# An expert's remaining tiles in a six-arm branch, with the arm told to TensorE beforehand

## The chip, the core and the metric

The kernel runs on one core of a Trainium2 chip. The core has five engines that work side by side and wait for each other by semaphores: TensorE (PE; its weight loads are listed apart as PEld), VectorE (DVE), ScalarE (ACT), GpSimd (POOL) and SyncE (SP). Each engine takes its instructions, branches among them, from its own queue. The time is in microseconds on the device, from one execution of the whole program; less is better.

## What is computed

Sliding-window causal attention (8 batches, 8 heads, 576 positions, head size 64, window 64) makes 4608 rows of 512. A mixture of 8 experts then works on them: each row goes to the one expert with the highest logit, and no row is dropped.

```python
scores = where(0 <= i - j < 64, q @ k.T / 8, -1e9)
x = (softmax(scores) @ v) -> [4608, 512]
logits = x @ w_gate                       # [4608, 8]
e = argmax(logits, 1);  gate = softmax(logits)[e]
out = gate * (relu(x @ w1[e]) @ w2[e])    # w1 512x1024, w2 1024x512, in float32
```

How many rows an expert gets is known only when the routing is done, on the chip.

## The kernel before

The attention runs first, over 16 units of two batches and two heads. Its rows go to memory (`x_dram`), their gates are folded in, and the routing (`choose`, `starts`, `slot_table`) builds a list of rows ordered by expert (`perm_i`). An expert's rows are handled in tiles of 256 slots (`TB`). A tile is either *full* (`hidden` and `output`: one level of Strassen-like products, seven for each of the two layers) or, where at most 160 slots are left, a *half tile* (`half_tile`: plain products on 160 slots).

`starts` (L215) works out for each expert how many full tiles (`fulls_i`) and how many tiles of any kind (`all_i`) it has, eight numbers each in `info_i`. `loads` (L870) brings them into registers of every engine. Expert 0 always has its first two tiles done ahead of the loop (`NE`), as `tile0` and `tile1`; each other expert has at least one, taken as full.

The order within the loop is written out by hand (`manual_schedule`). `body` (L481) is one tile. Its first steps belong to the tile before: `finish` (L422, the last three additions on VectorE) and `scatter` (L287, two indirect DMAs by GpSimd into the result). Then come, where given, sums of weights on GpSimd (`between`: four instructions at L139), the products, the transposes of the next tile's rows on VectorE (L311), and `gather` (L268, two indirect DMAs by GpSimd that bring the rows of the tile after the next). So the data of a tile are gathered two tiles ahead, and TensorE can begin a tile while VectorE finishes the one before.

For each expert the loop issues the loads of the next expert's weights on SyncE (L1060, L1061), does `body` for the first tile (not for expert 0), and calls `more` for the rest. `more(n)` (L1068) is a chain of nested conditions: is there a tile n (L1070)? Is it full (L1071)? If full, the body and then `more(n + 1)` inside; else the half tile and out. From the fourth tile on a loop takes over. Every engine goes through these branches on its own. Where a path is not taken, its semaphore counts are made up for at the branch (on GpSimd the records INC_SWDGE_SEM and the waits ahead of them), so that the code that follows can wait for one number whatever the path. Nothing in the nested conditions is announced to an engine ahead of the branch.

Of the kernel before, what the change touches and what calls it, by code (L numbers as in the profile page):

```python
# [13 lines left out]
I32 = mybir.dt.int32  # L14
AF = mybir.ActivationFunctionType
ALU = mybir.AluOpType
# [20 lines left out]
def kernel(  # L37
# [29 lines left out]
    NE = 2  # L67
# [3 lines left out]
    KT = 4  # L71
# [16 lines left out]
    wg = consts.tile([P, NG, GE], F32, name="wg")  # L88
    nc.gpsimd.memset(wg[:], 0.0)
    perm_i = consts.tile([P, NS], I32, name="perm_i")  # L90
    info_i = consts.tile([P, 2, E], I32, name="info_i")
    fulls_i, all_i = info_i[:, 0], info_i[:, 1]

    places_i = consts.tile([P, E + 1], I32, name="places_i")
    perm_e = consts.tile([P, NE * C], I32, name="perm_e")
# [119 lines left out]
    def starts():  # L215

        for got, slots in ((fulls_i, TB - 1 - HALF), (all_i, TB - 1)):
            V.tensor_scalar(out=got, in0=count[:], scalar1=float(slots), scalar2=float(TB), op0=ALU.add, op1=ALU.max)
            V.tensor_single_scalar(got, got, TB.bit_length() - 1, op=ALU.arith_shift_right)
        V.tensor_copy(out=nt[:], in_=all_i)  # L220
        V.tensor_tensor_scan(out=cum[:], data0=ones[:, 0:E], data1=nt[:], initial=0.0, op0=ALU.mult, op1=ALU.add)
        V.tensor_tensor(out=start[:], in0=cum[:], in1=nt[:], op=ALU.subtract)
        V.tensor_single_scalar(chunk0[:], start[:], float(C), op=ALU.mult)
# [273 lines left out]
    with tc.manual_schedule(), ExitStack() as held, ExitStack() as brief:  # L497
# [372 lines left out]
        def loads():  # L870

            both_ = lambda t: t[0:1].rearrange("p a e -> p (a e)")
            _, n = nc.values_load_multi_w_load_instructions(both_(info_i), min_val=0, max_val=NT // P)
            _, places = nc.values_load_multi_w_load_instructions(
                places_i[0:1, :], engines=(mybir.EngineType.Pool,), min_val=0, max_val=NTILE
            )
            return [(n[e], n[E + e], places[e]) for e in range(E)], places[E]

        def after(s, routing, bg):

# [173 lines left out]
    with tc.manual_schedule():  # L1054
        load_w1(1)
        load_w2(1)
        for e in range(E):
            fulls, tiles, first = regs[e]
            if 0 < e < E - 1:
                load_w1(e + 1)  # L1060
                load_w2(e + 1)  # L1061
            def place(i):
                i = nc.s_assert_within(
                    first + i, 0, NTILE - 1, skip_runtime_bounds_check_because="a tile with a token is one of the NTILE"
                )
                return bass.ds(i * C, C), bass.ds((i + 3) * C, C)

            def more(n, between=None):  # L1068

                with tc.If(tiles > n) as some_left:  # L1070
                    with tc.If(fulls > n, preferred_fallthrough_block=False) as full:  # L1071
                        body(e, *place(n), True, between)
                        if n + 1 < KT:
                            more(n + 1)
                        else:
                            with tc.For_i(KT, fulls) as i:
                                body(e, *place(i), True)
                            with tc.If(tiles > fulls):
                                body(e, *place(fulls), False)
                    with full.Else():  # L1080
                        body(e, *place(n), False, between)
                if between is not None:
                    with some_left.Else():
                        between()

            if e:
                body(e, *place(0), True, partial(sums_w2, e))
            more(1 if e else NE, partial(sums_w1, e + 1) if e + 1 < E else None)
        finish()
        scatter(perm_i[:, bass.ds(end * C, C)])  # L1090

# [27 lines left out]
```

## Time and profile before

| what | value |
|---|---|
| three runs | 742.86, 746.24 and 747.09 us; median 746.24 us |
| the profiled execution | 741.95 us, of which the profile's span is 740.2 us |
| granted TensorE clock, mean | 0.975 |
| attention, routing and the first two tiles of expert 0 | 0 to about 272 us |
| the expert loop | about 272 to 728 us |
| from TensorE's last product to the end | 728 to 740 us |
| PE, PEld, DVE, ACT, POOL busy | 94, 84, 67, 36, 48% of the span |

A line of a group or of the timeline reads: engine, line of the kernel, operation, what it writes and reads (partitions x elements), how often, and in brackets the idle time of the engine ahead of it with what released it. "issue" means that the engine waited for nothing that the profile shows. A q behind an engine's name means its queue's own instructions, branches among them, which are not counted as busy. TensorE's queue works ahead of its matmuls.

### The profile page before, as it was taken

Reading aid. Unit: us, or ns where it says so; the run is one execution under the profiler, and the core shown is the slowest. Engines: PE = TensorE matmul, PEld = TensorE weight load, DVE = VectorE, ACT = ScalarE, POOL = GpSimd, SP = SyncE. Lnnn points to the kernel's source line nnn. Section 1 sums busy time; section 2 is a strip of 40 time slices with the busy share of each in tenths; the row PEclk is TensorE's granted clock in tenths of the full one; section 3 lists DMA queues with packets and bytes.
Section 4 is the critical chain, followed back from the end, with each engine's and each line's share of the span. In section 5 each row is a group of like instructions: output and inputs, shape, how many; then the busy total and the mean of one; then the engine's idle time right before and its main releaser. Section 6 shows DMA issues by size and latency. Waiting matters only on the chain. (4 is left out here: it accounts for less than half of the span.)

```text
span 740.2 us, 18250 instructions
## 1 busy us (share of the span) xinstructions
PE 695.1 (94%) x6962; PEld 625.4 (84%) x6962; DVE 496.7 (67%) x1654; ACT 267.3 (36%) x676; POOL 355.7 (48%) x366
## 2 busy tenths in 40 slices
PE   4999999999799989999999999999899999989993
PEld 3888888888678978998999899899899899989892
DVE  2576898998848484765677568667466568556762
ACT  4788888897735111212122122112111222111220
POOL 5224659288680217676540555654167654262102
PEclk8899999999989999999999999999999999999997
DMA  8998879887524635336100630711422711101101
GB/s 160 218 210 188 182 179 228 192 212 214 176 55 143 205 109 180 127 107 228 59 29 31 220 124 18 271 59 43 174 110 78 253 60 28 61 9 59 33 27 57
DMA packets 137636, 94.68 MB, mean 128 GB/s; under 512 B 117072, under 2 KB 117072, under 8 KB 137490
## 3 DMA queue, kind: packets, MB, share of 16 engines
q1 hardware_dynamic: 127858, 62.16, 31.7%
q0 software_dynamic: 9056, 28.58, 11.8%
q10 hardware_dynamic: 576, 2.10, 1.0%
q8 instruction: 78, 1.28, 0.7%
q14 instruction: 68, 0.56, 0.3%
HBM read 73.94 MB, written 20.45 MB: 128 GB/s over the span
## 5 line engine op out<-in xcount | busy, mean ns | idle before, releaser
L311 DVE STREAM_TRANSPOSE v_m<-qk_m 32x256 f32<-32x256 f32 x320 | 139.3, 435 | 5.2 <-DMA qk_m<-x_dram,at_g 0.3
L340 PE MATMUL bank<-qk_m,s 128*128 128x128 f32 x1024 | 124.7, 278 | 0.6 <-issue 0.6
L271 POOL DMA_INDIRECT qk_m<-x_dram,at_g x42 | 45.0, 1072 | 165.0 <-DVE v_m L311 155.9
L340 PEld LDWEIGHTS bank<-qk_m,s 128*128 128x128 f32 x1024 | 120.6, 195 | 0.6 <-issue 0.6
L340 PE MATMUL bank<-qk_m,w 128*128 128x128 f32 x768 | 96.0, 279 | 11.8 <-issue 8.1
L340 PEld LDWEIGHTS bank<-qk_m,w 128*128 128x128 f32 x768 | 91.0, 194 | 15.9 <-issue 15.7
L652 ACT ACTIVATE pr<-pr,mx 128x128 f32<-128x128 f32 x288 | 89.7, 390 | 31.7 <-DVE mx L642 31.3
L642 DVE CUSTOM_DVE_ANT_0 pr<-bank,mask 128x128 f32<-128x128 f32 x288 | 64.4, 285 | 28.0 <-PE bank L629 26.7
L380 DVE TENSOR_TENSOR v_m<-bank,v_m 128x256 f32<-128x256 f32 x95 | 38.2, 420 | 55.3 <-PE bank L384 24.9
L291 POOL DMA_INDIRECT out_dram<-v_m,at_s x42 | 42.5, 1013 | 61.5 <-DVE v_m L380 47.2
L570 POOL COPY v_m<-v_m 64x520 f32<-64x520 f32 x32 | 19.8, 618 | 68.6 <-DMA v_m<-in_v_dram 58.3
L139 POOL TENSOR_TENSOR s<-w 128x1024 f32<-128x1024 f32 x22 | 52.2, 2373 | 0.0
L675 PEld LDWEIGHTS bank<-v_m,pT 128*64 128x64 f32 x1152 | 41.1, 140 | 10.9 <-DVE xs L689 4.8
L675 PE MATMUL bank<-v_m,pT 128*64 128x65 f32 x1152 | 47.8, 231 | 1.9 <-DVE xs L689 1.9
L347 ACT COPY qk_m<-bank 128x512 f32<-128x512 f32 x16 | 9.4, 586 | 108.2 <-PE bank L340 88.1
L384 PE MATMUL bank<-qkT_m,v_m 128*128 128x256 f32 x216 | 48.3, 379 | 0.0
L384 PEld LDWEIGHTS bank<-qkT_m,v_m 128*128 128x128 f32 x216 | 41.0, 190 | 5.5
L441 PEld LDWEIGHTS bank<-qk_m,w 128*128 128x128 f32 x320 | 45.1, 194 | 0.4
L441 PE MATMUL bank<-qk_m,w 128*128 128x160 f32 x320 | 45.3, 303 | 0.0
L629 PE MATMUL bank<-qkT_m 64*64 64x128 f32 x1152 | 44.8, 286 | 0.1
L596 PE MATMUL bank<-ident,qk_m 128*128 128x128 f32 x256 | 36.5, 287 | 8.0 <-POOL mask L518 4.9
L660 PE MATMUL bank<-ident,pr 128*128 128x128 f32 x288 | 43.8, 290 | 0.0
(174 smaller groups left out, 1254.7 us busy)
## 6 DMA issues: line engine op xcount, KB each, us to landing
w<-in_moe_w_dram SPq DMA_DIRECT2D x11, 2048.0 KB, 9.0
qk_m<-in_q_dram SPq DMA_DIRECT2D x72, 128.0 KB, 3.7
qk_m<-in_k_dram SPq DMA_DIRECT2D x72, 128.0 KB, 3.6
v_m<-in_v_dram SPq DMA_DIRECT2D x64, 128.0 KB, 4.2
qk_m<-in_moe_w_dram SPq DMA_DIRECT2D x3, 2048.0 KB, 15.6
x_dram<-xs POOLq DMA_DIRECT2D x6, 512.0 KB, 4.9
x_dram<-xs POOLq DMA_DIRECT2D x3, 768.0 KB, 5.2
w<-in_moe_w_dram ACTq DMA_DIRECT2D x4, 512.0 KB, 4.9
```

The source lines that it names most:

```text
L139: op()
L271: G.indirect_dma_start(out=xg[c], out_offset=None, in_=x_dram[:, :], in_offset=bass.IndirectOffsetOnAxis(ap=at_g[:, c : c + 1], axis=0),)
L291: put = G.indirect_dma_start(out=out[:, :], out_offset=bass.IndirectOffsetOnAxis(ap=at_s[:, c : c + 1], axis=0), in_=ys[c], in_offset=None ...
L311: V.transpose(out=xn[b * QD : (b + 1) * QD, :, :, a * QD : (a + 1) * QD].rearrange("p c g i -> p (c g) i"), in_=rows[a * QD : (a + 1) * QD ...
L340: nc.tensor.matmul(acc[:, f, :], lhsT=a[:, g, f * P : (f + 1) * P], rhs=b[:, g, :], start=(first and f == 0 and g == 0), stop=(g == HG - 1 ...
L384: nc.tensor.matmul(acc, lhsT=a[:, f, :], rhs=b[:, f, :], start=(start and f == 0), stop=(stop and f == HF - 1), skip_group_check=True,)
L441: nc.tensor.matmul(acc[:, i], lhsT=w1[:, g, f * P : (f + 1) * P], rhs=xq[:, g].rearrange("p c s -> p (c s)")[:, 0:HALF], start=(i + g == 0 ...
L629: nc.tensor.matmul(out_, lhsT=qT[rows, t, a * WINDOW : (a + 1) * WINDOW], rhs=rhs, start=True, stop=True, skip_group_check=True,)
L642: V.tensor_tensor_reduce(out=prs[h][:, m, :], in0=scs[h][:, m, :], in1=mask[:, m0 + m, :], scale=-scale, scalar=-2 * MASKED, op0=ALU.add, ...
L652: nc.scalar.activation(out=y, in_=y, func=AF.Exp, scale=-1.0, bias=mx[:, h, m : m + 1])
L660: nc.tensor.transpose(out=tr[:, m, :], in_=prs[h][:, m, :], identity=ident[:])
L675: nc.tensor.matmul(px[a * D : (a + 1) * D, h, m, :], lhsT=pTs[h][:, m, a * D : (a + 1) * D], rhs=vt[:, h, :], start=True, stop=True, skip_ ...
```

## The change

`starts` works out a third number for each expert, its *kind*: full tiles plus all tiles, less twice the tiles that are known beforehand, and at most 5. `loads` brings it in as a third group of eight registers. In the loop the chain of conditions gives way to a switch on the kind, whose arms hold the remaining tiles in a row, without a test between them: 0 none, 1 a half tile, 2 a full one, 3 a full and a half, 4 two full, 5 two full and then the old chain `more` for what is left. At the head of the expert, ahead of its first `body`, a `switch_hint` gives TensorE, and no other engine, the kind, with which it can name the arm before it comes to the switch. For expert 0 no `body` lies between the hint and the switch. In the built program each arm begins on each engine with a hint of the branch that leaves the arm. The sums of weights that `more` had as `between` go with the arm's first tile, or alone into arm 0. Semaphore counts are made up for within the arms (on GpSimd ahead of each indirect DMA in arms 1 to 4 and, in arms 0 to 2, once more at the end), up to the counts of arm 5.

```diff
-    info_i = consts.tile([P, 2, E], I32, name="info_i")
-    fulls_i, all_i = info_i[:, 0], info_i[:, 1]
+    KINDS = 6
+    info_i = consts.tile([P, 3, E], I32, name="info_i")
+    fulls_i, all_i, kind_i = (info_i[:, n] for n in range(3))
...
+        V.tensor_tensor(out=kind_i, in0=all_i, in1=fulls_i, op=ALU.add)
+        for es, known in ((slice(0, 1), NE), (slice(1, E), 1)):
+            V.tensor_scalar(
+                out=kind_i[:, es], in0=kind_i[:, es], scalar1=float(-2 * known), scalar2=float(KINDS - 1),
+                op0=ALU.add, op1=ALU.min,
+            )
...
-            return [(n[e], n[E + e], places[e]) for e in range(E)], places[E]
+            return [(n[e], n[E + e], n[2 * E + e], places[e]) for e in range(E)], places[E]
...
-            fulls, tiles, first = regs[e]
+            fulls, tiles, kind, first = regs[e]
...
-            def more(n, between=None):
+            def more(n):
 
-                with tc.If(tiles > n) as some_left:
+                with tc.If(tiles > n):
                     with tc.If(fulls > n, preferred_fallthrough_block=False) as full:
-                        body(e, *place(n), True, between)
+                        body(e, *place(n), True)
                         if n + 1 < KT:
                             more(n + 1)
                         else:
-                            with tc.For_i(KT, fulls) as i:
+                            with tc.For_i(n + 1, fulls) as i:
                                 body(e, *place(i), True)
                             with tc.If(tiles > fulls):
                                 body(e, *place(fulls), False)
                     with full.Else():
-                        body(e, *place(n), False, between)
-                if between is not None:
-                    with some_left.Else():
-                        between()
+                        body(e, *place(n), False)
 
+            engines = mybir.EngineType
+            hint = tc.switch_hint({engines.PE: kind}, KINDS, label=f"rest_{e}")
             if e:
                 body(e, *place(0), True, partial(sums_w2, e))
-            more(1 if e else NE, partial(sums_w1, e + 1) if e + 1 < E else None)
+            ahead = partial(sums_w1, e + 1) if e + 1 < E else None
+            known = 1 if e else NE
+            for arm in tc.Switch(kind, KINDS, hint=hint):
+                done = 0
+                for _ in range(min(arm // 2, 2)):
+                    body(e, *place(known + done), True, None if done else ahead)
+                    done += 1
+                if arm % 2 and arm < KINDS - 1:
+                    body(e, *place(known + done), False, None if done else ahead)
+                if arm == 0 and ahead is not None:
+                    ahead()
+                if arm == KINDS - 1:
+                    more(known + done)
```

## The prediction

> **What bounds the kernel now.** First the page's head and the work by stage, to see which engine has no slack; then the idle time of TensorE; then the branches themselves; then the places where another engine might become late.
>
> ```profile
> span 740.2 us, 18250 instructions
> PE 695.1 (94%) x6962; PEld 625.4 (84%) x6962; DVE 496.7 (67%) x1654; ACT 267.3 (36%) x676; POOL 355.7 (48%) x366
> ```
>
> In the expert loop (272 us to 728 us) PE is nearly full and no other engine is above some two thirds, so a microsecond in which PE stands still there is a microsecond of the result. PE's timeline, the lines with idle time:
>
> ```profile
> 295.39 2.02 PE L340 MATMUL bank<-qk_m,w 128*128 128x128 f32 x16 [1.47 <-DMA qk_m<-x_dram,at_g]
> 339.05 2.02 PE L340 MATMUL bank<-qk_m,w 128*128 128x128 f32 x16 [1.15 <-issue]
> ...
> 535.73 3.05 PE L340 MATMUL bank<-qk_m,w 128*128 128x128 f32 x16 [1.92 <-issue]
> ...
> 651.64 1.49 PE L340 MATMUL bank<-qk_m,w 128*128 128x128 f32 x9 [2.24 <-issue]
> 652.92 3.40 PE L340 MATMUL bank<-qk_m,s 128*128 128x128 f32 x16
> ```
>
> There are ten such lines at L340: 1.47, 1.15, 1.22, 0.57, 0.88, 1.92, 0.88, 0.53, 2.24 and 1.36, together 12.22 us. All stand at a tile's first or second product, where nearly nothing but control flow lies ahead. The branches of PE's queue, the first view of one stretch, the second of all executions of the line:
>
> ```profile
> L1071 PEldq COMPARE_BRANCH  x1: 4366/4366/4366, 290.2 to 290.2; - x1
> ...
> L1071 PEldq COMPARE_BRANCH  x17: 67/380/5446, 272.7 to 698.5; - x17
> L1070 PEldq COMPARE_BRANCH  x18: 68/78/4542, 272.6 to 729.5; - x18
> ```
>
> Most take 0.07 to 0.4 us; eleven of 35 take 3.3 to 5.4 us. Eight of these leave an expert (at 290.2, 334.2, 409.8, 461.1, 530.1, 576.2, 644.2, 724.6) and three step over an untaken block inside one (385.1, 487.6, 698.5). They are jumps to code that is not there yet: the page's queue 8 brings instructions in pieces of 1.28 MB/78, some 16 KB. PE's queue runs ahead of its matmuls (the branch at 290.2, the last matmul before it ending at 293.9), so 3.7 us of each are hidden and 0.5 to 1.9 us show. The 0.57 and 2.24 come a few matmuls after a landing, without a branch: the next piece was late too.
>
> **The change, part by part.** Tiles per expert, from the trace: half; full, half; three full; two full; two full, half; full, half; two full, half; three full. So arms 1, 1, 4, 2, 3, 1, 3, 4 run, never 0 or the nested rest in 5.
>
> *Jumps of PE.* For experts 1 to 7 PE gets the arm's address a whole full tile (24 us) ahead, and in the built program every arm opens on every engine with a hint of its own exit. The 4 us of fetching fit under either. The tests inside an expert are gone. I take the nine gaps after the first as gone: 12.22 - 1.47 = 10.75 us. The lower end is 0 (hints without effect), the upper 10.75.
>
> *Clock.* The gaps of 1.92 and 2.24 are each followed by a stretch at half clock (granted clock 0.57 in 536 to 540 and in 652 to 656): sixteen products take 3.40 where others take 1.95. Each costs about 1.6 us (1.0 + 0.6 over 535.73's two groups; 1.45 and a remainder): 3.2 us go with the gaps. [...]
>
> *End.* The end waits for the last gather, whose data nobody uses, on GpSimd, before the last additions:
>
> ```profile
> 726.27 1.89 PE L384 MATMUL bank<-w,v_m 128*128 128x256 f32 x8
> 731.78 1.27 DVE L380 TENSOR_TENSOR v_m<-bank,v_m 128x256 f32<-128x256 f32 x3 [6.15 <-DMA out_dram<-v_m,at_s]
> 732.15 0.18 POOL L288 COPY at_s<-perm_i 128x2 int32 x1 [6.90 <-DMA qk_m<-x_dram,at_g]
> 733.03 1.02 POOL L291 DMA_INDIRECT out_dram<-v_m,at_s  x1 [0.69 <-DVE v_m L380]
> 735.99 1.01 POOL L291 DMA_INDIRECT out_dram<-v_m,at_s  x1 [1.94 <-issue]
> ```
>
> That wait belongs to the skipped path of L1070, which makes up semaphore counts (2.24 us of counting at 729.4). Arm 4 has the full count and ends with a plain branch. Then the additions can end at 728.2 + 0.45, and the second scatter start 0.8 us after that, as in a middle tile (364.34 to 365.16), or 2.9, as now at the end, instead of at 735.99: 4.4 to 6.5 us. I take the middle, 5.5. Lower end 1: if VectorE's exit misses as at 725.2 to 729.7, it starts at 731.
>
> *Entries of the other engines.* VectorE, ScalarE, GpSimd and SyncE have no hint of the arm; its block lies apart from the switch. [...] Rows: VectorE's far jump at 410.4 went on at 414.1 (3.7 us), that at 725.2 at 729.7 (4.45); GpSimd's at 334.5 shows as 4.78 us below. What hides it on VectorE, at the entry to a full tile:
>
> ```profile
> 362.19 0.76 DVE L380 TENSOR_TENSOR v_m<-bank,v_m 128x256 f32<-128x256 f32 x2 [0.85 <-PE bank L384]
> 363.92 0.42 DVE L380 TENSOR_TENSOR v_m<-bank,v_m 128x256 f32<-128x256 f32 x1 [0.97 <-PE bank L384]
> ...
> 367.56 0.69 DVE L350 TENSOR_TENSOR qk_m<-bank,qk_m 128x512 f32<-128x512 f32 x1 [3.21 <-PE bank L340]
> ```
>
> 0.85 + 0.97 + 3.21 = 5.03 us of waiting for PE, and 0.8 more (its end at 368.25 to 369.07) before PE's fourth product needs the result. 4.2 us and the switch's few register steps fit; at 6 us five entries to full tiles would cost 0.2 each, at 5.45 nothing. In a half tile the waits are 0.92 + 0.90 + 2.61. ScalarE waits 6.88 us for its first product. SyncE next waits for PE's end of an expert's weights (issues at 284.96, 294.00, 328.99). Cost 0.
>
> *GpSimd's counting.* Arms 1 to 4 count ahead of each of a tile's four indirect DMAs, before only half tiles did: 48 steps for 20, at 0.44 to 1.23 us. They lie in its wait for VectorE's transposes, 142.7 us in 16 gathers. Cost 0; if the second gather came 1.2 late, it would still land (4.1 us after issue) well ahead of its transposes (360.0 and 368.2).
>
> *Expert 0.* Here the hint stands directly at the switch and nothing covers it. PE's branch at 272.6 was short; now some 4.3 us, against work until 275.1: 2 us of gap. GpSimd is worse. It has no slack between 275.5 and 291:
>
> ```profile
> 278.59 1.01 POOL L291 DMA_INDIRECT out_dram<-v_m,at_s  x1 [0.43 <-issue]
> ...
> 288.98 0.19 POOL L269 COPY at_g<-perm_i 128x2 int32 x1
> ...
> 290.76 0.96 POOL L271 DMA_INDIRECT qk_m<-x_dram,at_g  x1 [0.30 <-issue]
> ...
> 339.52 0.18 POOL L288 COPY at_s<-perm_i 128x2 int32 x1 [4.78 <-issue]
> ```
>
> Between lie four sums of 2.36. In the program PE's first product of expert 1, and of no other, waits for both of these gathers. They were there by 294.8; 4.2 to 4.65 us for the entry and 0.5 for the longer register load make it 299.3 to 299.9, against 295.39: 4.5 us, which takes in PE's own gap. PE then stands 3 to 4 us, and a half-clock stretch follows: 1.6. Together 6.1, ends 0 (fetch short) and 7.
>
> *Routing.* Three small VectorE instructions and 24 registers for 16: VectorE's load at 267.7 lasted 1.35 under its transposes, SyncE's 16 values 6.2 us long before its loads bind. 0 to 0.5; I take 0.3.
>
> **Sum.** -10.75 - 3.2 - 5.5 + 6.1 + 0.3 = -13.05 on an execution of 741.95 (span 740.2 and 1.75 around it): 728.9. The median of the runs, 746.24, is 4.3 above that execution; carried to it, 733.2, and I say 733.
>
> **Rivals.** (1) The entry of expert 0 costs little, because the arm's block is there: -13.05 - 6.1 = -19.15, so 727. For it: after most of GpSimd's branches the next step follows within 0.5 us. Against: those went to code nearby. (2) The hint holds for one kind of jump only. Exits only: the seven entries each show 1.13, the mean of the seven plain gaps (1.15, 1.22, 0.88, 1.92, 0.88, 0.53, 1.36): -13.05 + 7.9 = -5.15. Entries only: the exits keep their gaps (all but the 1.36) and the clock, about -1. So 741 to 745. (3) Slower: neither holds. No hint runs in this trace (all sit in the untaken loop), so nothing excludes it. Then there are eight misses more at the switch, one for each expert, and the exits stay: 7 x 1.13 - 1.36 + 6.1 - 1 = +11.6, so 758. It decides from the point at which an arm's first product starts over 1 us after the product before it.
>
> **How the numbers follow.** Forecast 0.57, (1) 0.17, (2) 0.13, (3) 0.13. The forecast's own range is 727 to 740. The range reaches to (1)'s lower bound (expert 0 free, end 6.5: -20.5, 726) less the 3.4 by which the lowest run lies under the median, 722, and over (2) to 746; it leaves out (3). About 0.5% (3.7 us) is what a measurement can tell: faster 0.79 (forecast, (1), a part of (2)), same 0.08, slower 0.13.
>
> **What would show it.** Right: no PE branch above 1 us from expert 1 on; idle lines at L340 only at experts 0 and 1; half clock gone near 536 and 652; the last additions within 1 us of PE's end; VectorE's entries 4 us late but its L350 still waiting for PE. Wrong: branches of 3 to 5 us at the switch, PE waiting for L350, or a next piece of code late inside the arms (0.5 to 2 us each), which no row of straight code here shows.

## The result and the profile after

The changed kernel is slower, by 1.1%. Its median is 750.75 us over 20 runs (745.65 to 755.3), against 742.14 us for the kernel before over 20 runs on the same chip (738.53 to 747.09): a ratio of 1.0109, 95% interval 1.009 to 1.0129. The forecast was 733 us, range 722 to 746. The profiled execution of the changed kernel took 752.25 us, its span is 750.5.

The page's head and TensorE's timeline, the lines with idle time in the loop:

```profile
span 750.5 us, 18401 instructions
PE 701.6 (93%) x6962; PEld 629.4 (84%) x6962; DVE 509.3 (68%) x1657; ACT 266.7 (36%) x676; POOL 358.5 (48%) x366
```

```profile
279.80 11.80 PE L448 MATMUL bank<-qk_m,w 128*128 128x160 f32 x64 [2.13 <-issue]
301.10 2.02 PE L347 MATMUL bank<-qk_m,w 128*128 128x128 f32 x16 [0.51 <-PE bank L466]
307.58 3.81 PE L347 MATMUL bank<-qk_m,s 128*128 128x128 f32 x32 [0.89 <-DVE qk_m L357]
318.67 2.73 PE L391 MATMUL bank<-s,qk_m 128*128 128x256 f32 x8 [1.97 <-POOL s L140]
355.26 3.81 PE L347 MATMUL bank<-qk_m,s 128*128 128x128 f32 x32 [1.24 <-DVE qk_m L357]
366.35 2.63 PE L391 MATMUL bank<-qkT_m,qk_m 128*128 128x256 f32 x8 [1.97 <-POOL qkT_m L140]
...
610.70 3.78 PE L391 MATMUL bank<-qkT_m,qk_m 128*128 128x256 f32 x8 [3.43 <-POOL qkT_m L140]
681.61 2.00 PE L391 MATMUL bank<-s,qk_m 128*128 128x256 f32 x8 [0.81 <-POOL s L140]
```

(L347, L391 and L448 are L340, L384 and L441 of the kernel before; L357 is L350, `u2`, a sum that VectorE forms for a full tile's fourth product; L387 is L380; L140 is L139.) In what follows an *entry* is the branch of the switch into an arm, an *exit* the branch that leaves the arm for the next expert. All the old gaps at a tile's first product are gone but for 0.51 us at expert 1; at expert 0's entry 2.13 us are new. In place of the old gaps stand two other waits, and both lie in an expert's *first* tile, the one that follows an exit: at the fourth product for `u2` from VectorE (4.8 us in four), and at the second output product for the four sums of the second weights from GpSimd (11.0 us in six). Behind some of these waits the clock is halved: at 610.70 eight products take 3.78 us where others take 2.0 (granted clock 0.50 from 609.9 to 616.7).

TensorE's own branches did what the change promised. Here all sixteen of them, entry and exit of eight arms (minimum, median and maximum in ns):

```profile
L1132 PEldq COMPARE_BRANCH  x16: 293/302/4225, 275.3 to 737.9; - x16
```

Single records: 4.2 us at expert 0's entry (hint and switch together there), 1.1 us at expert 7's entry, 2.0 to 2.8 us at the three exits from an arm of one half tile (experts 0, 1 and 5; hidden in the queue), 0.3 us at the others.

Where the time came from, worked out from the starts of the tiles in both traces:

| stretch | before | after | difference |
|---|---|---|---|
| up to the start of `tile0` | 215.27 | 217.32 | +2.05 |
| from there to the start of expert 1 | 80.12 | 83.78 | +3.66 |
| first tiles of experts 1 to 7, together | 180.23 | 197.30 | +17.07 |
| all other tiles | 252.54 | 243.03 | -9.51 |
| from TensorE's end to the end | 12.07 | 9.11 | -2.96 |
| span | 740.24 | 750.54 | +10.3 |

So the change gained in the arms and at the end, and lost more in the first tiles. The loss has its cause at the exit before, on VectorE and GpSimd, and reaches TensorE through the order of GpSimd's queue. First the kernel before, its GpSimd around expert 1's start, then the changed kernel, the same place:

```profile
290.76 0.96 POOL L271 DMA_INDIRECT qk_m<-x_dram,at_g  x1 [0.30 <-issue]
291.97 0.24 POOL L288 COPY at_s<-perm_i 128x2 int32 x1 [0.25 <-issue]
297.29 1.02 POOL L291 DMA_INDIRECT out_dram<-v_m,at_s  x1 [5.07 <-DVE v_m L380]
...
299.61 2.41 POOL L139 TENSOR_TENSOR s<-w 128x1024 f32<-128x1024 f32 x1
...
306.72 2.37 POOL L139 TENSOR_TENSOR s<-s,w 128x1024 f32<-128x1024 f32 x1
```

```profile
296.51 0.96 POOL L278 DMA_INDIRECT qk_m<-x_dram,at_g  x1 [0.30 <-issue]
302.40 0.18 POOL L295 COPY at_s<-perm_i 128x2 int32 x1 [4.92 <-issue]
306.83 1.02 POOL L298 DMA_INDIRECT out_dram<-v_m,at_s  x1 [4.25 <-DVE v_m L387]
308.16 1.00 POOL L298 DMA_INDIRECT out_dram<-v_m,at_s  x1 [0.30 <-issue]
309.16 2.40 POOL L140 TENSOR_TENSOR s<-w 128x1024 f32<-128x1024 f32 x1
...
316.28 2.34 POOL L140 TENSOR_TENSOR s<-s,w 128x1024 f32<-128x1024 f32 x1
```

Before, GpSimd went on within 0.25 us here (of its exits from half tiles only the one at 334.5 stood long, 4.78 us). After, its exit leads past the other arms, and it stands 4.92 us with nothing to wait for. VectorE stands too, 5.59 us where it stood 2.72 (first line before, second after; the second names TensorE's next product as releaser, but these additions need only the half tile's last one: before they ran 2.1 us after its end at 293.91 and ahead of the end of any product of expert 1, after 5.0 us behind its end at 300.59):

```profile
296.02 1.27 DVE L380 TENSOR_TENSOR v_m<-bank,v_m 128x256 f32<-128x256 f32 x3 [2.72 <-issue]
```

```profile
305.57 1.27 DVE L387 TENSOR_TENSOR v_m<-bank,v_m 128x256 f32<-128x256 f32 x3 [5.59 <-PE bank L347]
```

Behind that stands a chain: VectorE's exit and its last additions, `scatter` on GpSimd, which waits for them, then in the order of GpSimd's queue four sums of 2.36 us, and only then TensorE's second output product. The first of these sums starts 8.1 us into expert 1's first tile where it started 4.2 before, and at experts 2, 5 and 6 it is 8.3 to 9.3 for 4.1 to 4.7. The later of the two exits decides, and mostly that is VectorE's: GpSimd, through with its own exit, still waits 4.25, 1.12, 3.29, 4.16 and 3.65 us for VectorE's additions at experts 1, 2, 3, 5 and 7; at 4 the two come together, and only at 6 is GpSimd the last. In the kernel before the fourth sum ended 0.6, 0.3, 0.5, 0, 2.4, 0.2 and 4.0 us ahead of that product in experts 1 to 7 (309.1 against 309.7 in the first; the 0 is a wait of 0.52, here on its timeline):

```profile
480.53 1.99 PE L384 MATMUL bank<-qkT_m,qk_m 128*128 128x256 f32 x8 [0.52 <-POOL qkT_m L139]
```

There was no slack to speak of, and TensorE's queue itself had been held for 3.7 to 5.4 us at each exit, of which 0.5 to 1.9 us showed and delayed that product with all others. The change took TensorE's delay away and lengthened VectorE's at four of the five exits from half tiles (2.6 to 3.0 us became 5.2 to 5.7), and GpSimd's at most exits.

The groups of GpSimd's copies ahead of the scatter, of before and of after, give the total for entries and exits: time for which nothing but the queue itself held them ("issue") rose from 5.0 to 39.4 us, 33.1 of it at the eight exits.

```profile
L288 POOL COPY at_s<-perm_i 128x2 int32 x20 | 4.3, 217 | 31.2 <-DMA qk_m<-x_dram,at_g 18.9 <-issue 5.0 <-DMA out_dram<-v_m,at_s 4.6
```

```profile
L295 POOL COPY at_s<-perm_i 128x2 int32 x20 | 3.7, 186 | 45.2 <-issue 39.4 <-DVE v_m L387 5.8
```

### The profile page after: what moved, and what is told of

It reads as the page before. It is cut to its first block, busy times and chain, and to the rows that moved or that the text cites. A ratio compares the mean times of both kernels' runs of the same rounds, so it can differ in the third digit from the quotient of the medians.

```text
span 750.5 us, 18401 instructions
## 1 busy us (share of the span) xinstructions
PE 701.6 (93%) x6962; PEld 629.4 (84%) x6962; DVE 509.3 (68%) x1657; ACT 266.7 (36%) x676; POOL 358.5 (48%) x366
## 3 DMA queue, kind: packets, MB, share of 16 engines
q14 instruction: 149, 1.22, 0.5%
## 4 chain that ended last, share of the span: by engine, by line
PE 68%; DVE 8%; issue 8%; DMA 6%; POOL 6%; SPq 1%; ACT 1%; POOLq 0%; DVEq 0%; ACTq 0%
PE bank L391 22%; PE bank L347 18%; DMA out_dram<-v_m,at_s 5%; PE bank L448 5%; PE bank L682 4%; PE bank L636 4%; PE bank L667 4%; POOL qkT_m L140 3%; PE bank L603 3%; PE bank L466 2%; POOL s L140 2%; PE bank L719 2%; PE bank L707 2%; DVE pr L649 1%; DVE pT L669 1%
## 5 line engine op out<-in xcount | busy, mean ns | idle before, releaser
L347 PE MATMUL bank<-qk_m,s 128*128 128x128 f32 x1024 | 122.8, 276 | 4.8 <-DVE qk_m L357 4.8
L347 PEld LDWEIGHTS bank<-qk_m,s 128*128 128x128 f32 x1024 | 118.3, 192 | 5.5 <-issue 4.1
L347 PE MATMUL bank<-qk_m,w 128*128 128x128 f32 x768 | 93.9, 276 | 0.5 <-PE bank L466 0.5
L347 PEld LDWEIGHTS bank<-qk_m,w 128*128 128x128 f32 x768 | 90.7, 192 | 1.7 <-issue 0.9
L387 DVE TENSOR_TENSOR v_m<-bank,v_m 128x256 f32<-128x256 f32 x95 | 38.3, 421 | 76.6 <-PE bank L347 40.5
L140 POOL TENSOR_TENSOR s<-w 128x1024 f32<-128x1024 f32 x22 | 52.3, 2376 | 0.0
L682 PEld LDWEIGHTS bank<-v_m,pT 128*64 128x64 f32 x1152 | 40.9, 140 | 10.9 <-DVE xs L696 4.7
L448 PEld LDWEIGHTS bank<-qk_m,w 128*128 128x128 f32 x320 | 46.8, 201 | 3.0 <-issue 2.8
L448 PE MATMUL bank<-qk_m,w 128*128 128x160 f32 x320 | 47.2, 312 | 2.1 <-issue 2.1
L391 PE MATMUL bank<-qkT_m,v_m 128*128 128x256 f32 x216 | 48.3, 380 | 0.0
L391 PEld LDWEIGHTS bank<-qkT_m,v_m 128*128 128x128 f32 x216 | 41.0, 190 | 5.4
## 6 DMA issues: line engine op xcount, KB each, us to landing
w<-in_moe_w_dram SPq DMA_DIRECT2D x11, 2048.0 KB, 10.9
```

What stands on the lines that cost most here:

```text
L140: op()
L347: nc.tensor.matmul(acc[:, f, :], lhsT=a[:, g, f * P : (f + 1) * P], rhs=b[:, g, :], start=(first and f == 0 and g == 0), stop=(g == HG - 1 ...
L391: nc.tensor.matmul(acc, lhsT=a[:, f, :], rhs=b[:, f, :], start=(start and f == 0), stop=(stop and f == HF - 1), skip_group_check=True,)
L448: nc.tensor.matmul(acc[:, i], lhsT=w1[:, g, f * P : (f + 1) * P], rhs=xq[:, g].rearrange("p c s -> p (c s)")[:, 0:HALF], start=(i + g == 0 ...
L682: nc.tensor.matmul(px[a * D : (a + 1) * D, h, m, :], lhsT=pTs[h][:, m, a * D : (a + 1) * D], rhs=vt[:, h, :], start=True, stop=True, skip_ ...
```

## The experiments

Theory A: the loss is made at the exits; GpSimd's sums and VectorE's `u2` come late in the tile that follows. Rival B: it is made at the entries, where only TensorE had a hint. Rival C: GpSimd's additional counting of semaphores. Rival D: routing and register loads ahead of the loop. C and D have no run of their own; what the traces say of them stands in the section on the prediction. All ratios are to the kernel before, measured beside it on the same chip.

| run | what | ratio | 95% interval |
|---|---|---|---|
| after_again | the changed kernel once more | 1.009 | 1.0056 to 1.0124 |
| no_hint | without TensorE's hint | 1.0103 | 1.007 to 1.0135 |
| all_hint | VectorE and GpSimd told too | 1.0072 | 1.0037 to 1.0107 |
| sums_first | all sums ahead of the scatter | 0.9872 | 0.982 to 0.9924 |
| before_sums_first | the same in the kernel before | 1.0146 | 1.0102 to 1.0189 |
| w2_first | only the second weights' sums ahead | 0.9897 | 0.987 to 0.9924 |
| w2_first_no_hint | that, without TensorE's hint | 1.0012 | 0.999 to 1.0034 |
| u2_first | w2_first, and `u2` ahead of `finish` | 0.9876 | 0.9845 to 0.9907 |
| u2_first_hint0 | that, and expert 0's hint earlier | 0.9845 | 0.9798 to 0.9892 |
| before_late | kernel before, 4.7 us more on GpSimd | 1.066 | 1.0613 to 1.0706 |
| half_no_sums | no such sums from expert 3 on | 0.991 | 0.9874 to 0.9945 |
| five_arms | without the sixth arm | 0.9984 | 0.9953 to 1.0016 |
| reversed | six arms in the opposite order | 1.0042 | 1.0009 to 1.0074 |
| five_reversed | five arms in the opposite order | 1.001 | 0.9985 to 1.0035 |
| u2_reversed | u2_first_hint0 with the order of reversed | 0.9875 | 0.9842 to 0.9907 |

**The order of GpSimd's work (sums_first, before_sums_first).** The edit, the same in both kernels:

```diff
-        finish()
-        scatter(perm_i[:, last])
         if between is not None:
             between()
+        finish()
+        scatter(perm_i[:, last])
```

> The changed kernel with one exchange in body(): the four sums on GpSimd come ahead of finish() and scatter() in place of behind them, so that GpSimd does not wait for VectorE's late finish (3.6 us after an exit of kind 1) and two scatters (2.3 us) before it starts them. Theory A: they end 5 us earlier than PE needs them or about then, the 11.0 us of PE's waits at L391 for GpSimd fall under 2 us and the half-clock stretches behind them go (about 5 us in four); the 4.8 us for u2 stay: 735 to 740 us. Rivals (entries, counting, register loads): no change, 749 to 752.

> The same exchange in the kernel before, as a control. There PE waited for these sums for 0.5 us in all, because its own queue stood 3.3 to 5.4 us at each exit. Theory A: nothing to gain, 740 to 744 us, within 0.5% of before. If the order alone were worth the 10 us, apart from the switch: 730 to 735.

Measured 0.9872 and 1.0146. The exchange takes 2.4% from the changed kernel (1.0109 to 0.9872, some 18 us; a little more than expected), and TensorE waits for these sums nowhere any more; the first tiles fall from 197.3 to 185.5 us. It does not work by being a better order as such: in the kernel before it costs 1.5%, which neither side had expected. The reason shows in both, where GpSimd's sums run beside the four subtractions `sums_x` on VectorE (L336; L329 before), both of whose operands are in SBUF. In sums_first, VectorE and then GpSimd at expert 7's start:

```profile
648.78 7.52 DVE L336 TENSOR_TENSOR qk_m<-v_m,qk_m 128x256 f32<-128x256 f32 x3 [0.23 <-ACT qk_m L330]
656.22 2.56 DVE L336 TENSOR_TENSOR qk_m<-qk_m,v_m 128x256 f32<-128x256 f32 x1
```

```profile
648.69 2.35 POOL L140 TENSOR_TENSOR s<-w 128x1024 f32<-128x1024 f32 x1 [1.75 <-PE bank L466]
651.12 2.40 POOL L140 TENSOR_TENSOR s<-w,s 128x1024 f32<-128x1024 f32 x1
653.49 2.53 POOL L140 TENSOR_TENSOR s<-w 128x1024 f32<-128x1024 f32 x1
655.98 2.52 POOL L140 TENSOR_TENSOR s<-s,w 128x1024 f32<-128x1024 f32 x1
```

In the changed kernel the same four on VectorE, with GpSimd standing at its exit:

```profile
298.42 1.22 DVE L336 TENSOR_TENSOR qk_m<-v_m,qk_m 128x256 f32<-128x256 f32 x3 [0.23 <-ACT qk_m L330]
299.55 0.42 DVE L336 TENSOR_TENSOR qk_m<-qk_m,v_m 128x256 f32<-128x256 f32 x1
```

Three subtractions take 7.52 us in place of 1.22, and the fourth 2.56 in place of 0.42: some 2.5 us apiece, beside sums of 2.35 to 2.53. GpSimd's first sum starts at 648.69, VectorE's first subtraction at 648.78. TensorE then waits 2.31 and 3.07 us for VectorE. In the kernel before, where GpSimd mostly leaves a half tile at once, its early sums fall on these subtractions too (6.71 and 2.57 us at 542); in w2_first GpSimd's late exit keeps them apart at expert 1 (the subtractions from 299.98 take 1.22 and 0.42, the first sum starts at 303.70). With an operand in a bank there was no such rise: beside the sums from 309.16 on in the changed kernel, VectorE's additions of 128x512 with one operand in a bank took 0.69 us each (310.05, 311.69, 313.33, 315.00), the first one with both in SBUF 2.77 (316.39; the next of that form, at 319.81, behind the last sum, 0.68).

**Only the second weights' sums, with and without the hint (after_again, w2_first, w2_first_no_hint, no_hint).**

```diff
-    def body(e, last, after, full, between=None):
+    def body(e, last, after, full, between=None, early=None):
 
+        if early is not None:
+            early()
         finish()
...
-                body(e, *place(0), True, partial(sums_w2, e))
+                body(e, *place(0), True, None, partial(sums_w2, e))
```

> The changed kernel once more, beside the next three on the same chip. All theories: 1.009 to 1.013 of before, PE's waits for the sums on GpSimd 9 to 12 us, for u2 4 to 6 us.

> As the first exchange in the changed kernel, but for the sums of the second weights in an expert's first tile alone; the sums of the first weights, which stand in the arms, stay behind the scatter. Theory A: the waits of PE for GpSimd stay gone, and the lateness that the first exchange made in half tiles (their scatter and gather 9.5 us late; idle lines of 1.69, 2.31 and 3.07 us behind 580 us, the last with a half-clock stretch) goes too: 0.974 to 0.983 of before. If those lines had another cause: 0.985 to 0.990, as with the first exchange.

Measured 1.009, as expected, and 0.9897: faster than before, but short of the range expected, inside the one given for another cause, and not told apart from sums_first. GpSimd in w2_first at expert 1:

```profile
303.70 2.36 POOL L140 TENSOR_TENSOR s<-w 128x1024 f32<-128x1024 f32 x1 [4.65 <-issue]
...
310.75 2.35 POOL L140 TENSOR_TENSOR s<-s,w 128x1024 f32<-128x1024 f32 x1
313.05 0.18 POOL L295 COPY at_s<-perm_i 128x2 int32 x1
```

GpSimd's exit still misses (4.65 us), but the sums no longer wait for VectorE's additions and two scatters, and end at 313.1, 5 us before TensorE needs them. The first tiles of experts 1 to 7 take 179.1 us together, 18.2 less than in the changed kernel, and all other tiles 243.05, the same as there (243.03). So the place of these sums in the queue carries the whole of the loss. The idle lines that the expectation named are gone too. What is left in the first tiles is `u2`: 5.7 us in the four lines

```profile
309.31 3.81 PE L347 MATMUL bank<-qk_m,s 128*128 128x128 f32 x32 [1.54 <-DVE qk_m L357]
353.19 3.81 PE L347 MATMUL bank<-qk_m,s 128*128 128x128 f32 x32 [1.38 <-DVE qk_m L357]
545.09 3.81 PE L347 MATMUL bank<-qk_m,s 128*128 128x128 f32 x32 [1.82 <-DVE qk_m L357]
588.58 3.81 PE L347 MATMUL bank<-qk_m,s 128*128 128x128 f32 x32 [0.98 <-DVE qk_m L357]
```

These were the error in the expectation: sums_first had less of it in three of the four places (0.41, 0.29, 0.68 us).

```diff
-            hint = tc.switch_hint({engines.PE: kind}, KINDS, label=f"rest_{e}")
...
-            for arm in tc.Switch(kind, KINDS, hint=hint):
+            for arm in tc.Switch(kind, KINDS):
```

> The changed kernel without the hint to TensorE at the head of the first tile; everything else stays. Theory A (the loss is made at the arms' exits: GpSimd and VectorE miss there, and the four sums of the next expert's second weights and VectorE's u2 come late): the hint did its work, so each of the seven entries behind a first tile costs PE 3 to 5 us in its queue again, of which 1 to 2 us show as idle time; 7 to 14 us slower than the changed kernel, 758 to 765 us, while the waits for the sums on GpSimd stay near 11 us. Rival (the hint is not what keeps the entries short, the code is there anyway): PE's entries stay at 0.3 us and the time at 749 to 752.

Measured 1.0103, against 1.0109 and 1.009 with the hint: no difference that can be told (their intervals reach 1.5 to 2.5 us either way), so the expected 7 to 14 us did not come. But TensorE's branches were as expected, the median of the sixteen up from 302 ns, the entries 3.4 to 4.6 us each:

```profile
L1130 PEldq COMPARE_BRANCH  x16: 301/2939/4581, 274.1 to 740.2; - x16
```

and with idle time behind six of the seven, like

```profile
377.08 2.02 PE L347 MATMUL bank<-qk_m,w 128*128 128x128 f32 x16 [1.20 <-issue]
```

In the two profiled executions TensorE takes 446.0 us from the start of expert 1 to its end without the hint and 440.3 with it, but from `tile0` to expert 1, where the hint stands directly at its switch, 81.3 and 83.8. So a part of the hint's gain seems to go at expert 0, and the 5.6 us from there on are less than the 6.5 us of idle time at the six entries. The next run asks whether the late sums swallow some.

> The kernel w2_first without TensorE's hint. In the changed kernel the hint was worth nothing (1.0103 without, 1.0109 with it), although its entries cost 3.4 to 4.6 us of queue time without it and six of them showed idle time of 0.75 to 1.43 us, 6.5 us together. Theory A (what the hint saved was lost again because PE then came sooner to sums that were late): with the sums early the hint is worth 5 to 9 us, so 0.983 to 0.992 of before. Rival (the hint's gain is lost elsewhere): within 2 us of w2_first.

Measured 1.0012. Beside w2_first (0.9897, same chip) the hint is now worth 1.15%, some 8.5 us, as Theory A had it (the ratio itself came out above the range expected, as w2_first did). In the traces it is 10.9 us from expert 1 on (433.1 and 422.2), of which 8.7 in the first tiles with their entry gaps at the end (187.9 and 179.1), less 3.6 at expert 0 (80.1 and 83.7). One and the same hint is worth nothing that can be told or 8.5 us, by whether the sums are in time.

**Lateness without any switch, and no sums without any lateness (before_late, half_no_sums).**

```diff
     def sums_w2(e):
+        if e:
+            b11, b12 = w2q(e)[:2]
+            for _ in range(2):
+                G.tensor_tensor(out=s2s[e % NW][:, 0], in0=b12, in1=b11, op=ALU.subtract)
```

> The kernel before, without any branch changed; ahead of the four sums of an expert's second weights GpSimd forms the first of them twice more (2 x 2.37 = 4.7 us, the same result), about what an exit miss of GpSimd costs in the changed kernel. Theory A (these sums have next to no slack): PE waits for them 3 to 4.5 us in most of the seven first tiles, with half-clock stretches behind the longer waits: 18 to 32 us slower, 1.025 to 1.043. Rival (the sums have slack, and what is late in the changed kernel comes of something else): within 0.5% of before.

Measured 1.066, more than the upper end. TensorE's waits:

```profile
PE bank L388 <- POOL qkT_m L139: 17.7, 3, 6.0
PE bank L388 <- POOL s L139: 17.6, 4, 6.1
```

and one of them on TensorE's timeline:

```profile
373.76 3.78 PE L388 MATMUL bank<-qkT_m,qk_m 128*128 128x256 f32 x8 [5.62 <-POOL qkT_m L139]
```

Seven waits make 35.3 us; six have their products at half speed behind them (3.6 to 3.8 us for 1.9); one wait for `u2` and the slow products behind it make the rest of the 51 us by which the first tiles grew (231.4 against 180.2). The waits exceed 4.7 us in part because the last two of the six took 2.8 us for 2.37 (so at experts 1 and 2). So a delay of this size on GpSimd at this place, with not one branch altered, makes the kernel slower by more than the changed kernel is.

```diff
-                body(e, *place(0), True, partial(sums_w2, e))
+                body(e, *place(0), True, partial(sums_w2, e) if e < 3 else None)
```

> The changed kernel with the four sums of the second weights formed for experts 1 and 2 only; experts 3 to 7 multiply by the sums that stand there from two experts before, so part of the computation is left out. Theory A: the waits of PE for GpSimd at experts 1 and 2 stay (2.0 us each and the half clock behind them), those at experts 3 to 7 go (7.0 us of idle time and, at expert 6, a half-clock stretch): 9 to 12 us less than the changed kernel, 0.994 to 0.999 of before. Rival: the time stays at 1.008 to 1.013.

Measured 0.991, a little less than expected. The waits at experts 1 and 2 are as in the changed kernel (1.99 and 1.97 us), from expert 3 on there are none for GpSimd; the waits for `u2` fell as well (4.8 to 1.7 us), which the expectation had not counted.

**The entries (all_hint).**

```diff
-            hint = tc.switch_hint({engines.PE: kind}, KINDS, label=f"rest_{e}")
+            hint = tc.switch_hint({n: kind for n in (engines.PE, engines.DVE, engines.Pool)}, KINDS, label=f"rest_{e}")
```

> The changed kernel with the arm told to VectorE and GpSimd as well as to TensorE, at the same place. Rival B (the loss is made at the arms' entries, where VectorE misses for 2.9 to 4.3 us and GpSimd for 2.5 because they had no hint): their entries fall to some 0.3 us and the time to 740 to 745. Theory A: the entries fall too, but the waits of PE for the sums (11.0 us at L391) and for u2 (4.8 us at L347) stand in first tiles, which follow exits; these stay, and the time stays at 748 to 752.

Measured 1.0072, an interval that overlaps that of the changed kernel; Rival B's 740 to 745 us, beside 742.14 a ratio of 0.997 to 1.004, only touch the lower end of that interval. But the premise of both was not met. Of the seven hinted entries behind a first tile VectorE went on in 0.5 us at two and still took 2.6 to 3.6 at five, and GpSimd went on in 0.4 us at one. PE's waits for the sums (10.9 us) and `u2` (4.9 us) stood as they were. So the entries are only shown to be no cheaper this way, not what they would be worth if all held; that every wait of TensorE for another engine in the changed kernel's loop stands in a tile that follows an exit, and none in one that follows an entry, says that it is little for the tile itself. The entries reach further, though: in the changed kernel, at experts 1 and 5, VectorE's late entry holds the scatter of the half tile behind it, so that GpSimd's four sums there start 4.2 and 5.0 us into it in place of 2.4 and 2.5, and GpSimd comes later to its exit. What share of the lateness at experts 2 and 6 this is, no run shows.

**VectorE's u2, and expert 0's hint (u2_first, u2_first_hint0).**

```diff
         V.tensor_tensor(out=u2, in0=y, in1=p1, op=ALU.add)
+        if behind_u2 is not None:
+            behind_u2()
...
-        finish()
-        scatter(perm_i[:, last])
+        def done():
+            finish()
+            scatter(perm_i[:, last])
+
+        if early is None:
+            done()
...
-        form_all(hidden(e, blocks))
+        form_all(hidden(e, blocks, done if early is not None else None))
```

> The kernel w2_first, and in an expert's first tile VectorE forms u2 before the three last additions of the tile ahead (1.3 us with their waits); the scatter follows them. Theory A (after an exit VectorE is 3.6 to 5.5 us late and PE waits for u2, 4.5 to 4.8 us in four tiles of the runs so far): these waits fall under 1 us, 3 to 5 us less than w2_first, 0.968 to 0.979 of before. Rival (VectorE's lateness then shows in the next thing it owes PE, the transposes or the next additions): the same as w2_first.

Measured 0.9876, short of the range expected and not told apart from w2_first's 0.9897. The waits for `u2` did go (5.7 to 0.7 us), but 1.6 us came at an addition that VectorE owes TensorE later in the same tile (L370), and 1.9 us at expert 6's sums: the rival's outcome, in the main.

```diff
         regs, end = loads()
+        hints = [tc.switch_hint({engines.PE: regs[0][2]}, KINDS, label="rest_0")]
         for _ in tile1:
             pass
```

> The kernel u2_first, and the hint for expert 0 stands right behind the loads of the registers, ahead of the last products of its second tile, in place of directly at its switch. If it runs early enough, PE's entry at 275 us falls from 4.2 us to some 0.3, and the idle time of 2.1 us at L448 with it: 2 to 3 us less than u2_first. If the registers come too late, or TensorE is held for other reasons there (GpSimd's and VectorE's entries of 2.5 and 4 us at the same place): the same.

Measured 0.9845, on another chip than u2_first; the intervals overlap, and a difference of 2 to 3 us is too small to be told there. The mechanism shows in the trace, TensorE at expert 0's half tile:

```profile
273.85 3.56 PE L393 MATMUL bank<-qk_m,v_m 128*128 128x256 f32 x8 [3.40 <-DVE v_m L389]
277.24 8.86 PE L450 MATMUL bank<-qk_m,w 128*128 128x160 f32 x64
```

The branch took 0.46 us (4.2 in the changed kernel), the idle time of 2.13 us is gone, and the 64 products take 8.86 us in place of 11.80 in the changed kernel, where the granted clock was 0.50 up to 284 and 0.79 from there to 288. Up to the start of expert 1 this trace is 3.5 us shorter than that of u2_first (78.4 us from `tile0`, for 81.9), but 2.3 us go again in expert 1's first tile, where TensorE waits 3.17 us for VectorE at L370. This version is 1.55% faster than the kernel before.

**Why the exits miss (five_arms, reversed, five_reversed, u2_reversed).** five_arms has no arm for what is left after two full tiles, so it does the work of these inputs, whose kinds go up to 4, and no more.

```diff
-    KINDS = 6
+    KINDS = 5
...
-                if arm % 2 and arm < KINDS - 1:
+                if arm % 2:
...
-                if arm == KINDS - 1:
-                    more(known + done)
```

> The changed kernel without its sixth arm (the nested tests and the loop), which no expert of these inputs takes and which makes the arms' common distance longest. Theory A says only that exits jump out of the code at hand, so they go on missing: 1.006 to 1.013 of before, GpSimd's and VectorE's exits at 3 to 6 us. Rival (the distance or the padding makes the misses): GpSimd's exits fall to the 0.4 us of before, the waits for the sums go, and the time falls to 0.985 to 0.995.

Measured 0.9984, between the two. GpSimd's and VectorE's exits from the arm that is now last went on in 0.4 to 0.5 us, and GpSimd's exits of kind 3, the arm before it, cost 0.5 us where they had cost 4.6 and 1.7; but its exits of kind 1 stayed at 4.0 to 5.5 us, VectorE's of kind 1 and 3 at 2.2 to 5.8, and 6.9 us of waits for the sums stayed too. Expert 5 shows which of the two exits counts there. It follows an exit of kind 3, where GpSimd was ready at once, and yet its scatter stood for VectorE, and TensorE's wait for the sums is the 1.97 us of the changed kernel:

```profile
535.54 0.18 POOL L295 COPY at_s<-perm_i 128x2 int32 x1 [0.79 <-issue]
544.83 1.03 POOL L298 DMA_INDIRECT out_dram<-v_m,at_s  x1 [9.11 <-DVE v_m L387]
```

```profile
556.66 1.99 PE L391 MATMUL bank<-s,qk_m 128*128 128x256 f32 x8 [1.97 <-POOL s L140]
```

So with the sums behind the scatter, a cheap exit of GpSimd alone bought nothing at this expert. The tail fell to 7.9 us (9.1), since VectorE's last exit was one of the short ones.

The reversed kernels take KINDS - 1 less the kind as the index, and give the arms in that order:

```diff
+        V.tensor_scalar(
+            out=kind_i, in0=kind_i, scalar1=-1.0, scalar2=float(KINDS - 1), op0=ALU.mult, op1=ALU.add,
+        )
...
             for arm in tc.Switch(kind, KINDS, hint=hint):
+                arm = KINDS - 1 - arm
                 done = 0
```

> The changed kernel with its six arms in the opposite order, and nothing else: the arms of one half tile, of one full tile and so on now stand 5th, 4th, 3rd, the rest first. Distance decides (in five_arms the arms that had become the last two left GpSimd in 0.4 to 1.0 us, the others in 2.8 to 6.2): GpSimd's exits behind experts 0, 1 and 5 fall from 4.6 to 5.7 us to about 0.5 to 1, PE's waits for the sums at experts 1, 2 and 6 (7.4 us and the half clock behind them) go, and expert 4's exit (kind 3, arm 3) stays late, with 2 us of waiting at expert 5; 6 to 10 us less than the changed kernel, 0.995 to 1.002 of before. Rival (the half tile is too short for the hint at its head, whatever the distance): these exits stay at 4 to 6 us, 1.006 to 1.013.

> The five arms in the opposite order: the long rest is gone, so that arms stand closer together, and one half tile is the fourth of five. Distance decides (in the run reversed one arm's width was still that of the long rest): GpSimd's exits behind experts 0, 1 and 5, 4.0 to 5.5 us in five_arms, fall to about 0.5 to 1.0, what arm 3 showed there; kind 3, now arm 1, rises from 0.5 to 4 or 5; PE's waits for the sums at experts 1, 2 and 6 go and the time falls below five_arms, to 0.985 to 0.994 of before. Rival (the half tile is too short for its hint): they stay at 4 to 5.5 us, 0.996 to 1.002.

Measured 1.0042 and 1.001, with GpSimd's exits of kind 1 at 4.8 to 5.6 us and at 4.0 to 5.4. Moving the half tile's arm towards the exit did nothing for these exits, in either. (reversed as a whole lies 0.5 to 0.7% under the changed kernel; in its trace the first tiles are nearly the same, 196.9 us for 197.3, and the stretch from `tile0` to expert 1 is 80.1 for 83.8.) In five_reversed kind 3, now second, kept its 0.5 us on GpSimd, and kind 4, now first, rose from 0.5 to 4.2 and 5.0 us on VectorE. So kind 4's exit was cheap from the last arm and dear from the first. The time between the hint and the exit is short for kind 1 (16 to 21 us on GpSimd); but kind 4 in the changed kernel has 49 us and misses as well. Neither distance nor time alone accounts for these exits, and this stays open.

> The kernel u2_first_hint0 with its arms in the opposite order. There the sums and u2 are early and PE's waits behind experts 0, 1 and 5 are small already (0.4 to 3.2 us, 5 us in all), so distance is worth less here: 0 to 4 us less, 0.979 to 0.985 of before. Rival: the same or slower, since the arms of three full tiles now leave from far away, at experts 2 and 7, and at the end of the kernel the last scatters come up to 3 us later.

Measured 0.9875, a little above the range expected: no gain from the order of the arms can be told here either.

## Why the prediction was wrong

**Jumps of PE (-10.75) and Clock (-3.2): right in mechanism.** In the trace of before one packet of queue 8 (instructions, 0.02 MB) falls within each of the eleven long branches. In that of the changed kernel no branch of TensorE behind expert 0's entry was above 1.2 us, but for the three half-tile exits of 2.0 to 2.8, which its queue hid. Of the old gaps at L340 one of 0.51 us is left. All tiles but the first ones became 9.5 us shorter. The half-clock stretches near 536 and 652 are gone, but three new ones came at the new waits (granted clock 0.50 from 319.8 and 367.6 for 3.4 us each, from 609.9 for 6.8).

**The exits of VectorE and GpSimd, for which the sum has no term: the step that failed.** They were taken to cost nothing by the sentences in Jumps of PE, "every arm opens on every engine with a hint of its own exit. The 4 us of fetching fit under either". *Entries of the other engines* asks of their entries alone, and only *End* allows, as its lower end, that one exit of VectorE misses. The hint of the exit held for TensorE (0.3 us, 2.0 to 2.8 from the arms of one half tile): VectorE's exits cost 2.4 to 5.5 us and GpSimd's 1.4 to 5.7 (holes in their records), and in place of 0 the first tiles behind them became 17.07 us longer. For the entries a cost of 0 was right as far as TensorE's own waits go: VectorE's took 2.9 to 4.3 us against 3.7 to 4.45, and in the tiles that follow an entry TensorE did not wait for it. Why the exits differ from engine to engine and from arm to arm stays open (five_arms, reversed).

**The slack that was never looked up.** The prediction checked GpSimd's slack at expert 0 and in the arms (Counting), not in an expert's first tile, where 0 to 0.6 us is left in five of seven. The row that would have shown it stood in the profile before: TensorE's wait of 0.52 us for a sum at 480.53. It also overlooked that TensorE's own stall at each exit was a cover: with the 0.5 to 1.9 us of it that showed gone, GpSimd is that much later against TensorE even where it misses no more than before. The runs put the price of the late sums at 18.2 us in the first tiles (w2_first) and about 14 us of time (1.009 to 0.9897), more than the whole 1.1% that was lost. What makes the exits late on these two engines, and not on TensorE, no run shows.

**End (-5.5): mechanism right, size off.** The wait for the last gather went, but VectorE's exit missed 2.8 us, the case named as lower end. The tail gained 2.96 us; where that exit was short (five_arms) it gained 4.2.

**Expert 0 (+6.1): too dear.** 3.66 us in the profiled execution, 2.6 in after_again. TensorE's gap of 2.13 us and the half clock came; GpSimd's entry took 2.5 us and not 4.2 to 4.65, and that TensorE would stand for the late gather did not show, its first product of expert 1 waited 0.51 us for its own product ahead. (In the kernel before that product had waited for this gather until 295.39; it was not there "by 294.8".) The place of the hint seems to set this cost: with it at the switch the stretch from `tile0` to expert 1 took 81.9 to 84.0 us in the seven traces of six arms in their first order, without any hint 80.1 and 81.3, with the hint earlier 78.4, and in the kernel before 80.1.

**Counting (0): right, as far as the traces show.** No wait of TensorE leads back to these records, two indirect DMAs of a pair start no further apart in the loop than before (1.3 to 2.0 us for 1.3 to 2.1), and the sums' lateness goes with their order alone, the counting unchanged; no run left the counting out. **Routing (+0.3): not told.** The trace shows +2.05 us ahead of `tile0`, but this start lies between 215.3 and 219.5 us in all seventeen profiles (215.3 to 217.1 in the three without the switch), so the 2.05 cannot be put down to the change.

**The rivals.** The slower one had its place wrong: its mechanism was a hint that does not hold for TensorE. Nor does the half of it that was tried cost anything like the 25 us by which it lay above the forecast: without the hint of the entry the time is not told apart from that with it (no_hint). None of the cases let another engine's lateness grow out of TensorE's own gain, which is what decided. The sign "PE waiting for L350", listed as one of failure, did appear, though behind exits in place of entries.

## What to carry to other kernels

When a stall of the bounding engine is removed, every engine that worked in its shadow loses that much slack: take the instructions of each that the bounding engine waits for, and read how far ahead of need they end, at every place where the stall goes. A branch that one engine passes in 0.3 us (TensorE, but for 2.0 to 2.8 behind an arm of one half tile) can still hold the others: here VectorE stood 2.9 to 4.3 us at entries and 2.4 to 5.5 at exits, GpSimd 2.5 at expert 0's entry and 1.4 to 5.7 at exits, and the engine that was released last set the start of the work behind; so work that another engine needs should stand as early behind a jump as its data allow, and work that can wait should stand after it. A gain that does not show in the time may still be there, one engine further on: the same hint was worth nothing that could be told, and then 8.5 us.

## What the runs showed of the hardware that was not expected

- Exits of the arms opened with a hint on every engine, and took 0.3 us on TensorE (2.0 to 2.8 behind an arm of one half tile) but held VectorE for 2.4 to 5.5 us and GpSimd for 1.4 to 5.7. Hints of the entry to these two held in a part of the cases only (VectorE two of seven, GpSimd one of seven).
- In sums_first three float32 subtractions of 128x256 on VectorE with both operands in SBUF took 7.52 us, and a fourth 2.56, while GpSimd formed 128x1024 sums of 2.35 to 2.53 us; in the changed kernel, with GpSimd standing, they took 1.22 and 0.42. GpSimd's own sums rose from 2.36 to 2.53 us, 7%. So the early start on GpSimd made VectorE late there, and TensorE waited 2.31 and 3.07 us for it.
- Waits of TensorE of 1.97 us were followed by half clock in some places (2.73 and 2.63 us for eight products at 318.67 and 366.35, granted clock 0.50 from 319.8 and 367.6) and not in others (2.00 at 563.28, granted clock 1.00 from 563.2 to 565.4).
